# A fused attention and MLP kernel: rules of the build-time planner picked anew, first K and Q in one PSUM bank each, and the second MLP weight loaded at the third group of heads

## Chip, cores and metric

One core of a Trainium2 chip. The metric is the device time of one execution in microseconds (us). Before the change the median of three runs is 724.05 us (723.77 to 724.47).

## What is computed

Softmax attention over 2048 rows with 32 heads of 20 columns, an MLP with the Mish activation, and a gate per row that mixes the two. All inputs are bf16.

```python
x = A_x                                          # 1 x 2048 x 640
g = sigmoid((x * gate_w).sum(-1, keepdims=True))
q, k, v = split(x @ A_wqkv)                      # 32 heads, 20 columns each
p = softmax(q @ k.T * 20 ** -0.5)
a = (p @ v) @ A_wo
h = x @ B_w1 + B_b1
b = (h * tanh(softplus(h))) @ B_w2
return g * a + (1 - g) * b
```

## The kernel before

Heads go in blocks of four (p = 0 to 7) and query rows in chunks of 512 (qc = 0 to 3): 32 "groups" of one block and one chunk. In a group the keys come in 16 "sets" of 128 rows. A set has four score matmuls, one per head, on 32 rows of the array each, so up to four of them run side by side. The scores lie transposed (keys on the partitions) in PSUM, one bank of 512 columns per head and set.

The exponential is taken in two ways. ScalarE takes most: `emit_exp` (L1315) turns two or three neighbouring banks into bf16 in the ring E. VectorE takes the rest by a power trick (`power_of`, L474): one multiply-add into int16 whose bits are a bf16 power of two. Such a set gets two further copies, shifted by an integer add on VectorE (`shift`, L605) or GpSimd (`part`, L573), which are multiplied with scaled values VD. So a set on VectorE costs three value products (`emit_pv`, L1358) instead of one. Values are summed over all sets of a group in bank 7 and normalised (`normalise`, L1380 to L1410), and stored to `o_dram`.

Between scores and values TensorE is given "chains": projections of Q, K and V, both MLP products and the output projection, in pieces of four 32-column matmuls (`product`, L638), each chain with a start and a due time in units of groups.

The order on each engine is made when the program is built: a planner steps through a model of the engines and writes out the instructions in the order in which its engines become free (`step_pe`, `step_act`, `step_dve`, `step_pool`). On the chip each engine runs its list in order and waits on semaphores. The planner's thresholds are fields of `rule`; the table PLAN (L175 to L228) changes them as groups pass: `prog[0]` is the number of sets drawn, over 16, and an entry at 5.0 takes effect at the sixth group. Some of the fields: LOW (how little recent PE work counts as dry), DQ, DQ3, DQ4 (how many powers may queue on VectorE), NOPEN and LEAD (how many sets VectorE may hold open and take of a group), PS and PB (which shifts go to GpSimd, up to which backlog), WAIT1 and WAIT2 (priorities on VectorE), MERGE (two powers in one instruction).

Loads go through two DMA queues: SyncE's (nearly all) and, in the opening, ScalarE's. SyncE issues in order, with eight semaphores in rotation, so that an issue waits until the one eight places before it has landed. In the opening (L315 to L343) the first rows of x, the first K and Q weights (`load_first`, `w_top`) and V weights (`wv0`) are loaded, then the rest of x, weight strips `ws`, `wv`, the MLP's first weight in tiles `w1t`, and at L343 its second weight `w2_sb` (1920 KB; the profile calls the tile w_sb). Behind that on SyncE's queue come zeros for `o_dram` (L1500), the padding rows of K to `k_dram` (L708), Q and K strips to DRAM (L745) and the loads of each group's query tile qT from `q_dram` (L780).

The first projections are written out by hand (L1456 to L1492): transposes of x through banks 0, 3, 6, 2, then K and Q for the first 512 rows, each as ten matmuls of 256 columns into two banks (K 1 and 4, Q 5 and 0), after which VectorE copies one half and ScalarE the other. The first scores need both halves of Q.

At the end, `normalise` of the last group sets `closing`, and while it is set VectorE takes only work of the first priority (L1735).

Of the kernel before, what the change touches and what calls it, by code (L numbers as in the profile page):

```python
# [64 lines left out]
def kernel(  # L65
# [109 lines left out]
    PLAN = {  # L175
        0.0: {'AHEAD': 5000.0, 'BEHIND': 6000.0, 'D2': 1.0, 'DQ': 2, 'DQ3': 0, 'DQ4': 0, 'ETIGHT': 1, 'HEAT': 0.7, 'HROOM': 100.0, 'KEEP3': 3, 'LEAD': 5, 'LOW': 0.5, 'MARGIN': 0.0, 'MERGE': 0, 'NEAR': 99, 'NOPEN': 5, 'PAIR': 0, 'PB': 3000.0, 'PS': 0, 'PVMAX': 4, 'Q3': 3, 'ROOM': 200.0, 'SWTH': 250.0, 'TWO': 9, 'VF': 0, 'VMIN': 1, 'WAIT1': 0.0, 'WAIT2': 6000.0, 'WAITU': 0.0},
        0.5: {'DQ4': 1, 'NEAR': 9, 'WAIT2': 100000.0},
        1.5: {'DQ3': 3, 'ETIGHT': 0, 'HEAT': 0.9, 'VMIN': 3},
# [1 line left out]
        2.5: {'AHEAD': 1000.0, 'Q3': 2},  # L180
        3.5: {'AHEAD': 2000.0, 'NEAR': 7, 'Q3': 3, 'SWTH': 520.0, 'WAIT1': -2000.0},
        4.0: {'MARGIN': 30.0, 'NEAR': 99, 'PVMAX': 2, 'VF': 2, 'VMIN': 1},
        4.5: {'ETIGHT': 1, 'TWO': 2, 'VMIN': 3},
        5.0: {'KEEP3': 1, 'LEAD': 4, 'LOW': 0.47, 'NOPEN': 4, 'Q3': 1, 'SWTH': 600.0, 'WAIT2': 3000.0},
        5.5: {'HROOM': -100.0, 'KEEP3': 3, 'LOW': 0.53, 'NEAR': 12, 'PVMAX': 3, 'VMIN': 2},
        6.0: {'PVMAX': 2},
        6.5: {'HEAT': 0.7, 'PS': 2},
        7.0: {'DQ3': 2, 'NOPEN': 5, 'TWO': 9, 'VMIN': 1},
        7.5: {'PB': 6000.0},
        8.0: {'LEAD': 6, 'WAIT2': 30000.0},  # L190
        8.5: {'HROOM': 100.0, 'MERGE': 1, 'NEAR': 9, 'Q3': 3, 'VF': 0, 'WAITU': -200000.0},
        9.0: {'D2': 0.5, 'HEAT': 0.8, 'MERGE': 0, 'WAITU': 100000.0},
        9.5: {'AHEAD': 3000.0, 'MERGE': 1, 'SWTH': 250.0, 'WAIT1': 0.0},
        10.0: {'PVMAX': 4, 'VF': 2},
        10.5: {'HEAT': 0.9},
        11.0: {'KEEP3': 1, 'ROOM': 300.0},
        11.5: {'KEEP3': 2, 'ROOM': 100.0},
        12.0: {'D2': 0, 'DQ': 1, 'LOW': 0.41, 'MERGE': 0, 'SWTH': 450.0},
        12.5: {'NOPEN': 3, 'Q3': 1},
        13.0: {'Q3': 3},  # L200
        14.0: {'HROOM': -200.0, 'LOW': 0.47, 'WAIT2': 100000.0},
        14.5: {'NOPEN': 2},
        15.0: {'HEAT': 0.7},
        15.5: {'HEAT': 0.9},
        16.0: {'DQ3': 0, 'DQ4': 0, 'HROOM': -100.0},
        17.0: {'PB': 3000.0},
        17.5: {'D2': 0.5, 'PB': 6000.0, 'TWO': 2},
        18.0: {'ROOM': 200.0},
        19.0: {'LOW': 0.6, 'NOPEN': 5},
        19.5: {'DQ3': 2, 'DQ4': 3, 'ETIGHT': 0, 'KEEP3': 1, 'LOW': 0.53, 'TWO': 1},  # L210
        20.0: {'DQ4': 1, 'MARGIN': 60.0, 'MERGE': 1, 'TWO': 2, 'WAIT1': -2000.0, 'WAITU': 0.0},
        20.5: {'NEAR': 99, 'PB': 3000.0, 'SWTH': 380.0},
        21.0: {'DQ4': 2, 'KEEP3': 3, 'NEAR': 7, 'PVMAX': 3},
        21.5: {'ETIGHT': 1, 'MERGE': 0, 'PB': 6000.0, 'Q3': 2, 'WAIT2': 30000.0},
        22.0: {'HROOM': 0.0, 'ROOM': 100.0},
        23.0: {'HROOM': -200.0, 'TWO': 1},
        23.5: {'PVMAX': 2},
        24.0: {'MARGIN': 30.0, 'NOPEN': 2, 'TWO': 9},
        25.0: {'NOPEN': 4, 'PB': 1500.0, 'PVMAX': 4, 'ROOM': 200.0, 'SWTH': 520.0, 'WAIT2': 100000.0},
        25.5: {'LEAD': 5, 'PB': 3000.0, 'WAIT2': 3000.0},  # L220
        26.0: {'HROOM': 100.0, 'ROOM': 100.0, 'TWO': 2},
        26.5: {'HROOM': -200.0, 'PVMAX': 2},
        27.0: {'KEEP3': 2, 'WAIT1': 0.0, 'WAITU': 100000.0},
        27.5: {'LOW': 0.44, 'PVMAX': 4, 'Q3': 3},
        28.0: {'DQ': 2, 'KEEP3': 3, 'MARGIN': 0.0},
        28.5: {'LOW': 0.38, 'TWO': 9, 'WAIT2': 30000.0},
        29.5: {'DQ': 1, 'DQ4': 1, 'NOPEN': 2, 'PS': 0, 'Q3': 1, 'WAIT2': 100000.0},
# [91 lines left out]
    nc.scalar.dma_start(out=w_top[:, :, :], in_=wrows[:, :, D + KTOP : 2 * D])  # L319
# [1 line left out]
    nc.sync.dma_start(out=wv0[:, :, 0 : 4 * DH], in_=wrows[:, :, 2 * D : 2 * D + 4 * DH])
# [43 lines left out]
    def pad_copy(eng, dst, src):  # L365
        eng.tensor_copy(
            out=dst[:, :, :, 0:DH], in_=src.rearrange("p k (h d) -> p k h d", d=DH)
        )
# [1003 lines left out]
    def normalise(G, ready):  # L1372
# [2 lines left out]
        st = {}  # L1375

        def a(t):
            closing[0] = G == NG - 1
# [1 line left out]
            nc.vector.transpose(out=st["T1"][:, :, :].rearrange("p b r -> p (b r)"), in_=acc[:, :])  # L1380

# [97 lines left out]
    qT[0] = qTb[0]
    h_ = QC // 2  # L1480
    for w, dst, two in ((wkp, kT[0], (1, 4)), (wqp, qT[0], (5, 0))):
        for kt in range(KT):
            for h in range(2):
                nc.tensor.matmul(
                    allb[:, two[h], 0:h_],
                    lhsT=w[:, kt, :, :].rearrange("p h d -> p (h d)"),
                    rhs=xT[:, kt, h * h_ : (h + 1) * h_],
                    start=(kt == 0),
                    stop=(kt == KT - 1),
                )  # L1490
        nc.vector.tensor_copy(out=dst[:, 0:h_], in_=allb[:, two[0], 0:h_])
        nc.scalar.copy(out=dst[:, h_:QC], in_=allb[:, two[1], 0:h_])  # L1492
# [389 lines left out]
```

## Time and profile before

| | |
|---|---|
| median of the runs | 724.05 us |
| the profiled execution | 725.01 us |
| its span, from the first to the last instruction | 723.2 us |
| granted TensorE clock, mean | 0.999 |

The profile is of one execution. Busy times are per engine; a line such as L1315 is a line of the kernel before. Rows of a group give line, engine, operation, output<-input, shape and count, then busy time and mean duration of one (ns), then the engine's idle time ahead of them and who ended it. Rows of the timeline give start and length in us, and in brackets the idle time ahead with what ended it. Matmul ends are modelled, so the distance between starts says more than a duration.

### The profile page before, as it was taken

The page shows a single profiled execution, that of the slowest core. Times are in us where ns is not written, and L with a number is a line of the kernel's source. Part 1 is how long each engine was busy: PE and PEld are TensorE (multiplying, and loading weights), DVE is VectorE, ACT ScalarE, POOL GpSimd, SP SyncE. Part 2 cuts the span into 40 slices and gives each one's busy share as a digit, 9 for nine tenths or more (in the row PEclk, how much of TensorE's full clock was granted, in tenths as well). Part 3 has the DMA queues.
Part 4 walks back from the last instruction along what each step waited for, and adds up shares of the span by engine and source line. Part 5 has one row for each costly group of instructions (what it writes and reads, how often), then busy time and mean ns, then how long its engine had stood idle before and what let it go on. Part 6 is the DMA issues. An engine that isn't in the chain of part 4 may idle for free.

```text
span 723.2 us, 24705 instructions
## 1 busy us (share of the span) xinstructions
PE 706.3 (98%) x10256; PEld 232.5 (32%) x10256; DVE 619.6 (86%) x1042; ACT 704.3 (97%) x735; POOL 430.4 (60%) x697
## 2 busy tenths in 40 slices
PE   8899999999999999999999999999999999999997
PEld 4433332222222443332332222222243333333332
DVE  5389999887788779889988899898889988988997
ACT  6899999999999999999999999999999999999996
POOL 2002675565797767778787778667984456663000
PEclk9999999999999999999999999999999999999999
DMA  9511122122321201111131223231231131132111
GB/s 246 178 22 38 30 56 44 33 62 59 85 43 32 68 27 28 14 32 27 50 84 34 41 47 70 60 67 38 44 57 31 34 50 35 29 60 45 20 36 38
DMA packets 123313, 37.87 MB, mean 52 GB/s; under 512 B 90880, under 2 KB 122640, under 8 KB 123200
## 3 DMA queue, kind: packets, MB, share of 16 engines
q1 hardware_dynamic: 121600, 35.80, 22.8%
q8 instruction: 80, 1.31, 0.7%
q10 hardware_dynamic: 1600, 0.49, 0.3%
q14 instruction: 33, 0.27, 0.1%
HBM read 22.29 MB, written 11.48 MB: 47 GB/s over the span
## 4 chain that ended last, share of the span: by engine, by line
PE 62%; ACT 23%; issue 5%; DVE 4%; SPq 2%; DMA 2%; POOL 0%; ACTq 0%; POOLq 0%
PE Sp L1265 22%; ACT E L1315 20%; PE Sp L1358 20%; PE Sp L638 20%; DVE T L474 2%; ACT big L926 1%; DMA w_sb<-in_B_w_dram 1%; DVE T L605 1%; SPq L291 1%; SPq L304 1%; DMA big<-in_A_x_dram 1%; PE Sp L1822 0%; SPq L708 0%; SPq L324 0%; ACT L1315 0%
## 5 line engine op out<-in xcount | busy, mean ns | idle before, releaser
L1315 ACT ACTIVATE E<-Sp 128x1024 bf16<-128x1024 f32 x717 | 672.6, 1077 | 6.3 <-PE Sp L1265 5.9
L573 POOL TENSOR_TENSOR T<-T,step_t 128x256 int32<-128x256 int32 x652 | 401.1, 649 | 107.9 <-PE Sp L1358 71.5
L474 DVE TENSOR_SCALAR T<-Sp 128x512 int16<-128x512 f32 (+1 forms) x587 | 389.1, 686 | 62.3 <-PE Sp L1265 57.7
L1265 PE MATMUL Sp<-qT,kT 32*128 32x512 bf16 x2048 | 290.9, 384 | 8.0 <-ACT E L1315 3.7
L1265 PEld LDWEIGHTS <-kT 32*128 32x128 bf16 x2048 | 74.5, 91 | 267.0 <-issue 262.0
L1358 PE MATMUL Sp<-E,VA 128*21 128x512 bf16 x1456 | 138.0, 383 | 0.4 <-DVE T L1380 0.4
L1401 POOL TENSOR_TENSOR T<-T,rec 128x320 bf16<-128x320 f32 x31 | 25.1, 809 | 167.0 <-DVE rec L1394 140.0
L1358 PE MATMUL Sp<-T,VD 128*21 128x512 bf16 x1184 | 112.2, 382 | 0.5 <-DVE T L605 0.5
L605 DVE TENSOR_SCALAR T<-T 128x2048 int16<-128x2048 int16 x133 | 105.2, 797 | 1.5 <-PE Sp L1358 0.5
L638 PE MATMUL Sp<-xT,w1t 128*32 128x512 bf16 x960 | 76.8, 383 | 0.2
L638 PE MATMUL Sp<-w_sb,big 128*32 128x320 bf16 x1536 | 74.3, 301 | 0.3 <-DVE st L742 0.3
L1358 PEld LDWEIGHTS <-VA 128*21 128x21 bf16 x2048 | 44.4, 90 | 72.5 <-issue 64.5
L1358 PE MATMUL Sp<-T,VA 128*21 128x512 bf16 x592 | 57.4, 383 | 0.0
L638 PE MATMUL Sp<-xT,ws 128*32 128x512 bf16 x720 | 55.9, 382 | 0.5 <-DVE T L474 0.5
L638 PEld LDWEIGHTS <-big 128*32 128x32 bf16 x1536 | 35.4, 96 | 25.9 <-issue 15.8
L1358 PEld LDWEIGHTS <-VD 128*21 128x21 bf16 x1184 | 28.4, 90 | 37.6 <-issue 32.2
L892 DVE TENSOR_SCALAR big<-Sp,b1f 128x512 bf16<-128x512 f32 x48 | 35.6, 742 | 2.1 <-PE Sp L638 1.9
L638 PE MATMUL Sp<-wv,xT 128*32 128x81 bf16 (+2 forms) x960 | 34.6, 258 | 1.3 <-DVE T L474 1.3
L638 PE MATMUL Sp<-wo_sb,od 128*32 128x320 bf16 (+1 forms) x608 | 32.3, 302 | 0.0
L742 DVE CAST st<-Sp 128x512 bf16<-128x512 f32 x36 | 24.5, 681 | 5.3 <-PE Sp L638 5.3
L638 PEld LDWEIGHTS <-w1t 128*32 128x32 bf16 x960 | 19.0, 94 | 26.3 <-issue 22.4
L826 DVE CAST VA<-Sp 128x80 bf16<-128x80 f32 (+2 forms) x48 | 16.2, 372 | 10.1 <-PE Sp L638 10.1
(74 smaller groups left out, 205.7 us busy)
## 6 DMA issues: line engine op xcount, KB each, us to landing
w1t<-in_B_w_dram SPq DMA_DIRECT2D x24, 320.0 KB
q_dram<-st SPq DMA_DIRECT2D x20, 128.0 KB
out_dram<-ot SPq DMA_DIRECT2D x16, 160.0 KB
qT<-q_dram SPq DMA_DIRECT2D x124, 20.0 KB
o_dram<-T SPq DMA_DIRECT2D x120, 20.0 KB
kT<-k_dram SPq DMA_DIRECT2D x28, 80.0 KB
k_dram<-st SPq DMA_DIRECT2D x16, 128.0 KB
big<-in_A_x_dram SPq DMA_DIRECT2D x3, 640.0 KB
```

The lines of the kernel that those rows point to most:

```text
L291: eng.dma_start(out=t[:, :, :], in_=wrows[:, :, c0 : c0 + P])
L474: nc.vector.tensor_scalar(out=dst.bitcast(I16), in0=src, scalar1=inv_sqrt_dh * LOG2E * 128.0, scalar2=127.0 * 128.0 + BETA, op0=ALU.mult, ...
L573: nc.gpsimd.tensor_tensor(out=tile_[:, :].bitcast(I32)[:, k * n : (k + 1) * n], in0=d["T"][:, :].bitcast(I32)[:, k * n : (k + 1) * n], in1 ...
L605: nc.vector.tensor_scalar(out=tile_[:, :].bitcast(I16), in0=d["T"][:, :].bitcast(I16), scalar1=float(SHIFT[i]), scalar2=None, op0=ALU.add,)
L638: nc.tensor.matmul(out_[k : k + 32], lhsT=lhsT[:, k : k + 32], rhs=rhs, tile_position=(0, k), **kw)
L742: nc.vector.tensor_copy(out=res["st"][:, :], in_=ps[:, :])
L826: nc.vector.tensor_copy(out=VA[:, sts[i], h0 : h0 + nh, 0:DH], in_=ps[:, i, 0:n].rearrange("p (h d) -> p h d", d=DH),)
L892: nc.vector.tensor_scalar(out=big[:, slot.tag, (ft % 2) * QC : (ft % 2 + 1) * QC], in0=ps[:, :], scalar1=b1f[:, ft : ft + 1], scalar2=None ...
L1265: nc.tensor.matmul(ps_cols, lhsT=kT[p][32 * t_ : 32 * t_ + 32, j * P : (j + 1) * P], rhs=qT[G][32 * t_ : 32 * t_ + 32, :], tile_position=( ...
L1315: nc.scalar.activation(E[:, x : x + n, :], ps, ACT.Exp, scale=inv_sqrt_dh,)
L1358: nc.tensor.matmul(acc[32 * t_ : 32 * t_ + DH + 1, :], lhsT=lhsT, rhs=rhs, start=(pv_done[G] == 0), stop=(pv_done[G] == pv_total[G] - 1), ...
L1401: nc.gpsimd.tensor_tensor(out=T2[i][:, :].rearrange("p (b r) -> p b r", r=32)[:, :, 0:DH], in0=st["T1"][:, :, 0:DH], in1=st["rec"][:, :].u ...
```

## The change

1. PLAN is replaced whole: all fields of `rule` as before, other values at other groups (52 entries before, 59 after; those at 0.0 and 0.5 are the same).
2. First K and Q: five matmuls of 512 columns each into one bank (6 for K, 2 for Q); VectorE and ScalarE still copy one half each, now out of the same bank.
3. `w_top` moves from ScalarE's queue to SyncE's, `wv0` from SyncE's to ScalarE's, behind Q's weights.
4. `w2_sb` is not loaded in the opening but by an event once more than two groups' sets have been drawn.
5. `closing` is taken out.

```diff
     PLAN = {
...
         0.5: {'DQ4': 1, 'NEAR': 9, 'WAIT2': 100000.0},
-        1.5: {'DQ3': 3, 'ETIGHT': 0, 'HEAT': 0.9, 'VMIN': 3},
-        2.0: {'DQ4': 2, 'NEAR': 5, 'PS': 1, 'ROOM': 100.0, 'VMIN': 2, 'WAITU': 100000.0},
...
+        1.0: {'DQ4': 3, 'VMIN': 2, 'WAITU': 100000.0},
+        1.5: {'DQ4': 2, 'PS': 2, 'PVMAX': 3},
...
     load_first(1, nc.sync)
-    nc.scalar.dma_start(out=w_top[:, :, :], in_=wrows[:, :, D + KTOP : 2 * D])
     load_first(0, nc.scalar)
-    nc.sync.dma_start(out=wv0[:, :, 0 : 4 * DH], in_=wrows[:, :, 2 * D : 2 * D + 4 * DH])
+    nc.sync.dma_start(out=w_top[:, :, :], in_=wrows[:, :, D + KTOP : 2 * D])
+    nc.scalar.dma_start(out=wv0[:, :, 0 : 4 * DH], in_=wrows[:, :, 2 * D : 2 * D + 4 * DH])
...
     load_w1(1)
-    nc.sync.dma_start(out=w2_sb[:, :, :], in_=B_w2.rearrange("(ft p) c -> p ft c", p=P))
...
-    closing = [False]
...
-            closing[0] = G == NG - 1
...
-            closing[0] = False
...
+    sb = [bank_ap(g, [P, QC]) for g in (6, 2)]
     kT[0] = kTb[0]
     qT[0] = qTb[0]
-    h_ = QC // 2
-    for w, dst, two in ((wkp, kT[0], (1, 4)), (wqp, qT[0], (5, 0))):
+    for w, dst, k in ((wkp, kT[0][:, 0:QC], 0), (wqp, qT[0][:, :], 1)):
         for kt in range(KT):
-            for h in range(2):
-                nc.tensor.matmul(
-                    allb[:, two[h], 0:h_],
-                    lhsT=w[:, kt, :, :].rearrange("p h d -> p (h d)"),
-                    rhs=xT[:, kt, h * h_ : (h + 1) * h_],
-                    start=(kt == 0),
-                    stop=(kt == KT - 1),
-                )
-        nc.vector.tensor_copy(out=dst[:, 0:h_], in_=allb[:, two[0], 0:h_])
-        nc.scalar.copy(out=dst[:, h_:QC], in_=allb[:, two[1], 0:h_])
+            nc.tensor.matmul(
+                sb[k][:, :],
+                lhsT=w[:, kt, :, :].rearrange("p h d -> p (h d)"),
+                rhs=xT[:, kt, 0:QC],
+                start=(kt == 0),
+                stop=(kt == KT - 1),
+            )
+        h_ = QC // 2
+        nc.vector.tensor_copy(out=dst[:, 0:h_], in_=sb[k][:, 0:h_])
+        nc.scalar.copy(out=dst[:, h_:QC], in_=sb[k][:, h_:QC])
...
+    def load_w2():
+        nc.sync.dma_start(out=w2_sb[:, :, :], in_=B_w2.rearrange("(ft p) c -> p ft c", p=P))
+
     events = [
+        (lambda t: prog[0] > 2.0, lambda t: load_w2()),
...
-            if it[1] <= t and (it[0] == 0 or not closing[0]) and (it[6] is None or it[6](t)):
+            if it[1] <= t and (it[6] is None or it[6](t)):
```

More of the change, by code (lines that the diff above doesn't have):

```diff
@@ L177 @@
         0.5: {'DQ4': 1, 'NEAR': 9, 'WAIT2': 100000.0},
-        1.5: {'DQ3': 3, 'ETIGHT': 0, 'HEAT': 0.9, 'VMIN': 3},
-        2.0: {'DQ4': 2, 'NEAR': 5, 'PS': 1, 'ROOM': 100.0, 'VMIN': 2, 'WAITU': 100000.0},
[L180 to L227, printed above, removed]
+        1.0: {'DQ4': 3, 'VMIN': 2, 'WAITU': 100000.0},
+        1.5: {'DQ4': 2, 'PS': 2, 'PVMAX': 3},
+        2.0: {'DQ4': 1, 'PS': 1, 'PVMAX': 4, 'VF': 1, 'WAIT1': -2000.0},
+        2.5: {'Q3': 2},
+        3.0: {'DQ3': 2},
+        3.5: {'VF': 2, 'WAIT1': 2000.0, 'WAITU': 0.0},
@@ new lines @@
+        4.0: {'ROOM': 100.0},
+        4.5: {'D2': 0.5, 'ETIGHT': 0, 'MERGE': 1},
+        5.0: {'DQ4': 0, 'LEAD': 4, 'LOW': 0.47, 'MERGE': 0, 'NEAR': 99, 'NOPEN': 4, 'PS': 0, 'Q3': 1, 'SWTH': 600.0, 'VMIN': 3, 'WAIT2': 3000.0},
+        5.5: {'D2': 1.0, 'DQ3': 3, 'MARGIN': 100.0, 'WAIT1': -2000.0},
+        6.5: {'HEAT': 0.9, 'HROOM': -200.0, 'LEAD': 6, 'MARGIN': 0.0, 'PB': 6000.0, 'PS': 1, 'VMIN': 2},
+        7.0: {'MARGIN': 30.0},
+        7.5: {'VMIN': 1},
+        8.0: {'HEAT': 0.8, 'PS': 2, 'PVMAX': 2, 'Q3': 3, 'WAIT2': 100000.0},
@@ new lines @@
+        8.5: {'D2': 0, 'DQ3': 2, 'NEAR': 7},
+        9.0: {'DQ3': 1, 'WAIT2': 3000.0},
+        9.5: {'DQ3': 2, 'HROOM': 0.0, 'PVMAX': 4, 'WAIT1': 2000.0, 'WAIT2': 100000.0},
+        10.0: {'DQ3': 1},
+        10.5: {'MARGIN': 150.0, 'VF': 0},
+        11.0: {'LEAD': 5},
+        11.5: {'D2': 0.5, 'DQ': 1, 'DQ3': 0, 'MARGIN': 0.0, 'PB': 3000.0, 'PVMAX': 3},
+        12.0: {'NOPEN': 3, 'VF': 1},
+        12.5: {'VF': 2},
+        13.5: {'MERGE': 1, 'NOPEN': 4, 'PB': 6000.0, 'SWTH': 380.0},
+        14.0: {'PVMAX': 4, 'TWO': 0},
@@ new lines @@
+        14.5: {'HROOM': -100.0, 'LEAD': 6, 'MERGE': 0, 'PS': 1, 'Q3': 2, 'TWO': 9},
+        15.0: {'PS': 2},
+        15.5: {'D2': 1.0, 'PB': 3000.0},
+        16.0: {'DQ3': 3, 'HEAT': 0.9, 'NEAR': 5, 'NOPEN': 5, 'WAIT2': 30000.0},
+        16.5: {'LEAD': 5},
+        17.0: {'HEAT': 0.8, 'VMIN': 3},
+        17.5: {'D2': 0, 'KEEP3': 1, 'NEAR': 7, 'WAIT1': -2000.0},
+        18.0: {'D2': 1.0, 'HROOM': -200.0, 'KEEP3': 2, 'LOW': 0.5, 'NEAR': 9, 'PVMAX': 2},
+        18.5: {'KEEP3': 3, 'SWTH': 300.0},
@@ new lines @@
+        19.0: {'LOW': 0.6, 'MARGIN': 100.0, 'MERGE': 1, 'VMIN': 1, 'WAIT2': 3000.0},
+        19.5: {'DQ3': 0},
+        20.0: {'Q3': 1},
+        20.5: {'DQ4': 3, 'WAITU': -200000.0},
+        22.0: {'SWTH': 450.0, 'WAIT1': 0.0},
+        22.5: {'AHEAD': 2000.0, 'ETIGHT': 1, 'KEEP3': 2, 'LEAD': 6, 'WAIT2': 100000.0},
+        23.0: {'NEAR': 5, 'Q3': 2},
+        23.5: {'WAITU': 100000.0},
+        24.0: {'DQ3': 2, 'DQ4': 1},
+        24.5: {'NEAR': 7, 'PVMAX': 3, 'TWO': 1},
+        25.0: {'ETIGHT': 0, 'ROOM': 200.0},
@@ new lines @@
+        25.5: {'DQ4': 0},
+        26.0: {'Q3': 3},
+        26.5: {'D2': 0.5, 'DQ': 2, 'ETIGHT': 1, 'HROOM': 0.0, 'LOW': 0.56, 'WAIT2': 3000.0},
+        27.0: {'ETIGHT': 0, 'Q3': 2, 'WAIT2': 6000.0},
+        27.5: {'AHEAD': 5000.0, 'LOW': 0.41, 'MARGIN': 30.0, 'WAITU': -200000.0},
+        28.0: {'DQ': 3, 'LOW': 0.53, 'MARGIN': 60.0, 'MERGE': 0, 'ROOM': 100.0},
+        28.5: {'AHEAD': 1000.0, 'DQ3': 1, 'KEEP3': 1, 'MARGIN': 100.0, 'PVMAX': 2, 'SWTH': 300.0},
+        29.0: {'MARGIN': 30.0, 'PVMAX': 4, 'SWTH': 380.0},
@@ L228 @@
+        29.5: {'NOPEN': 2, 'TWO': 0, 'VF': 1},
+        30.5: {'DQ': 1, 'ETIGHT': 1, 'LOW': 0.41, 'PS': 1, 'VF': 2},
+        31.0: {'PS': 0, 'PVMAX': 2},
+        31.5: {'BEHIND': 3000.0, 'DQ4': 1, 'ETIGHT': 0, 'HROOM': 100.0, 'LEAD': 5},
     }
```

## The prediction

> **What bounds the kernel now.** I read the first page, then the stretches, then the chain of waits, then single pieces of the timeline.
>
> ```profile
> span 723.2 us, 24705 instructions
> PE 706.3 (98%) x10256; PEld 232.5 (32%) x10256; DVE 619.6 (86%) x1042; ACT 704.3 (97%) x735; POOL 430.4 (60%) x697
> PE 62%; ACT 23%; issue 5%; DVE 4%; SPq 2%; DMA 2%; POOL 0%; ACTq 0%; POOLq 0%
> ```
> ```profile
> 300.00:400.00 100.00, 99.23 (x1456) 30.94 (x1452) 88.44 (x143) 99.84 (x109) 78.61 (x126) 1.00 0.20 42
> 600.00:700.00 100.00, 99.58 (x1541) 33.80 (x1541) 91.83 (x154) 100.00 (x109) 42.34 (x68) 1.00 0.20 38
> 661.00:700.00 39.00, 38.92 (x618) 13.54 (x614) 37.33 (x65) 39.00 (x43) 0.73 (x1) 1.00 0.17 38
> ```
>
> The columns of the stretches are length, then busy time (with instructions) of PE, PE's weight loads, DVE, ACT and POOL, then the granted clock, DMA share and GB/s. TensorE and ScalarE are both full at a granted clock of 1.00, and the chain passes from one to the other: 62% on PE, 23% on ACT. A shorter order has to take work from both. VectorE stands close behind (92 of 100 us, and 37.3 of the last 39).
>
> **The exponentials (the rules).** From here on I compare the order of instructions in the two built programs. The new rules give 150 sets to VectorE's power trick instead of 148, so ScalarE gets 688 exponentials of 1024 columns (693 now), 24 of 1536 (23) and none of 512 (1).
>
> ```profile
> L1315 ACT ACTIVATE E<-Sp 128x1024 bf16<-128x1024 f32 x693 | 644.4, 1064 | 6.2 <-PE Sp L1265 5.9 <-PE Sp L1358 0.2
> L1315 ACT ACTIVATE E<-Sp 128x1536 bf16<-128x1536 f32 x23 | 34.2, 1487 | 0.1
> L1315 ACT ACTIVATE E<-Sp 128x512 bf16<-128x512 f32 x1 | 0.7, 667 | 0.0
> ```
>
> Consecutive ones overlap, so busy time over count is the price: 644.4/693 = 0.93 us for 1024 columns, 1.49 for 1536, 0.67 for 512. ScalarE's sum is -5 x 0.93 + 1.49 - 0.67 = -3.83 us.
>
> **TensorE (the rules).** Up to four small matmuls run side by side, so I count slots of four and read the distance between starts.
>
> ```profile
> 59.83 0.40 PE L1358 MATMUL Sp<-T,VD 128*21 128x512 bf16 x4
> 60.06 0.39 PE L1358 MATMUL Sp<-E,VA 128*21 128x512 bf16 x4
> 60.27 0.39 PE L1358 MATMUL Sp<-T,VA 128*21 128x512 bf16 x4
> 60.59 0.39 PE L1265 MATMUL Sp<-qT,kT 32*128 32x512 bf16 x4
> 60.92 0.29 PE L638 MATMUL Sp<-wv,xT 128*32 128x240 bf16 x4
> ```
>
> A slot of values after a slot of values comes 0.21 to 0.23 us later (I use 0.22), but the way into the scores costs 0.32 (60.27 to 60.59) and the way out 0.33. A visit to the scores therefore costs 0.32 + 0.33 - 0.22 = 0.43 us. The new order has 728 score slots instead of 739; 13 of those it loses stood directly behind another score slot (15 left of 28), so it has 2 visits more (713 for 711). Two more sets with two shifted copies each add 4 slots of values (812 for 808). Filler slots (projections, MLP, output) keep their number. Sum: -13 x 0.22 + 2 x 0.43 + 4 x 0.22 = -1.1 us.
>
> Which saving counts? Where PE sets the pace 1.1, where ACT does 3.8. I weigh them by the chain, 62 to 23: 0.73 x 1.1 + 0.27 x 3.83 = 1.8 us. Ends: -1.1 and -3.8.
>
> **The opening.** Loads and first projections of now:
>
> ```profile
> 1.65 0.43 SPq L298 DMA_DIRECT2D wf<-in_A_wqkv_dram  x1
> 1.65 0.46 ACTq L319 DMA_DIRECT2D w_top<-in_A_wqkv_dram  x1
> 2.12 0.53 SPq L321 DMA_DIRECT2D wv<-in_A_wqkv_dram  x1
> 6.06 0.22 DVE L1474 COPY wkp<-w_top 128x240 bf16<-128x240 bf16 x1
> 7.20 0.27 DVE L366 COPY wqp<-wf 128x400 bf16<-128x400 bf16 x1 [0.91 <-DMA wf<-in_A_wqkv_dram]
> 7.52 1.27 PE L1484 MATMUL Sp<-xT,wqp 128*128 128x256 bf16 x10
> 8.71 0.42 DVE L1491 CAST qT<-Sp 128x256 bf16<-128x256 f32 x1 [0.71 <-PE Sp L1484]
> 8.82 0.37 ACT L1492 CAST qT<-Sp 128x256 bf16<-128x256 f32 x1 [0.77 <-PE Sp L1484]
> 9.24 0.40 PE L1265 MATMUL Sp<-qT,kT 32*128 32x512 bf16 x4 [0.46 <-ACT qT L1492]
> ```
>
> Five matmuls of 512 columns stand for ten of 256: the same columns, cost 0. But the two halves of Q are now copied side by side out of two banks (8.71 and 8.82). In the changed program both lie in one bank, and ScalarE's copy waits for VectorE's: 8.82 + 0.42 + 0.37 + two hand-overs of about 0.05 (9.19 to 9.24) = 9.71 for the first score instead of 9.24, +0.48 us. K's pair is serial too, but its copies lie under Q's matmuls (1.27 us). The Trainium skill, "PSUM — Partial Sum Buffer", section on bank collisions, says that ScalarE and VectorE must not read one bank at the same partitions at once, reads against reads included. By it the 0.48 cannot be won back by dropping the wait; without it the copies would overlap and cost 0. The trace, with two banks, cannot show a collision.
>
> w_top moves from ScalarE's queue to SyncE's, behind wf: issued at 2.12 instead of 1.65. Q's weights move up a place on ScalarE's queue, and the V weights go behind them. K now waits for w_top. If it comes no later, 0 (PE has no idle before 7.52, so Q's earlier weights win nothing). If it comes as late as the last of the four today (7.20), VectorE copies at 7.20 instead of 6.06, and K and Q run 1.1 us later. I take +0.3, two thirds of the 0.47 by which the issue moves. Everything behind the first score is in order on PE, so I let the opening's +0.8 stand; 0 if a later load hides it.
>
> **w_sb.** It is on the chain now:
>
> ```profile
> 18.91 10.30 DMA w_sb<-in_B_w_dram
> SPq L708 <- DMA w_sb<-in_B_w_dram: 3.6, 1, 3.6
> 32.76 1.39 SPq L780 DMA_DIRECT2D qT<-q_dram  x4
> 35.21 0.71 PE L1265 MATMUL Sp<-qT,kT 32*128 32x512 bf16 x2 [0.84 <-DMA qT<-q_dram]
> 36.88 1.94 ACT L1315 ACTIVATE E<-Sp 128x1024 bf16<-128x1024 f32 x2 [1.40 <-PE Sp L1265]
> ```
>
> The transfer keeps SyncE's fourth K store waiting 3.6 us, this the second group's query load behind it (32.76), TensorE waits 0.84 us for that, and ScalarE 1.40. Without w_sb ahead of it the load is issued some 4 to 5 us earlier and both waits go: -1.4, the longer of them, as exponentials are what runs behind. Next late would be VectorE's powers for the same scores; if those hold PE, the gain is 0.
>
> In its new place the load's single issue stands on SyncE behind the first group's four stores, ahead of a K store, a Q store, the fourth group's four query loads and the second group's four stores.
>
> ```profile
> 54.10 2.89 SPq L1434 DMA_DIRECT2D o_dram<-T  x4
> 48.87 10.43 ACT L1315 ACTIVATE E<-Sp 128x1024 bf16<-128x1024 f32 x11
> ```
>
> That is about 57 us; with 10.3 us it lands by 67.3, and the query load (2.4 us from 32.76 to 35.2) by about 70 to 72. In the new order w_sb stands at the 47th exponential and the fourth group's first score at the 72nd: 25 x 0.95 = 23.7 us later, about 81. The cover is some 9 us of scores and values, cost 0; were it gone, the rest of the 10.3 would fall on TensorE. Its own reader comes much later, with the MLP.
>
> **The tail.** Removing "closing" lets VectorE take other work in the last normalisation; there is none left: 0.
>
> ```profile
> 712.51 2.46 DVE L605 TENSOR_SCALAR T<-T 128x2048 int16<-128x2048 int16 x4
> 713.40 0.10 PEld L1358 LDWEIGHTS <-VA 128*21 128x21 bf16 x4 [0.98 <-issue]
> 715.46 0.72 DVE L1380 STREAM_TRANSPOSE T<-Sp 128x512 f32<-128x512 f32 x1 [0.50 <-PE Sp L1358]
> ```
>
> Now four shifts are left for VectorE at the end, and PE waits. In the new order the last two are issued before the last exponential, and output slots fill the wait. I take -0.3 (half the first gap), between -0.8 and +0.3 (two filler slots too many).
>
> **Sum.** -1.8 + 0.5 + 0.3 - 1.4 - 0.3 = -2.7 us on this execution's 725.01 us (span 723.2 and 1.8 around it): 722.3. The runs shown have a median 0.96 below it, 724.05; on that scale 721.3.
>
> **Rivals.**
> 1. *ScalarE alone sets the pace* and PE's waits shrink with it: -3.8 + 0.8 - 1.4 - 0.8 = -5.2, 718.8. For it: ACT at 99.8 to 100 in every stretch. Against: the chain is on PE for 62%.
> 2. *VectorE comes late* (slower). Its work grows:
>
> ```profile
> L474 DVE TENSOR_SCALAR T<-Sp 128x512 int16<-128x512 f32 x582 | 383.1, 681 | 62.1 <-PE Sp L1265 57.5 <-POOL T L573 0.6
> L474 DVE TENSOR_SCALAR T<-Sp 128x1024 int16<-128x1024 f32 x5 | 6.1, 1216 | 0.2 <-PE Sp L1265 0.2
> L605 DVE TENSOR_SCALAR T<-T 128x2048 int16<-128x2048 int16 x133 | 105.2, 797 | 1.5 <-PE Sp L1358 0.5
> ```
>
> 578 single powers for 582 (0.66 each), 11 pairs for 5 (1.22), 135 shifts for 133 (0.79): -2.6 + 7.3 + 1.6 = +6.3 us. A power that is late keeps a bank, and so the scores behind it. If all 6.3 reach the path where the savings should be, the time is 6.3 + 0.8 - 1.4 - 0.3 = +5.4, 729.5; with half, +2.3, 726.3. It decides from about 2.4 of the 6.3 on (+2.4 - 0.9 = +1.5). For it: 92% busy late in the kernel. Against: 62 us of idle before its powers.
> 3. *The opening gives it back*: w_top as late as 7.20 and PE held by the powers where w_sb held it: -1.8 + 0.5 + 1.1 + 0 - 0.3 = -0.5, 723.5, no change.
> 4. *w_sb only moves its stall*: the fourth group's query load waits for it. With no cover, 10.3 us less what the old place cost: 721.3 + 10.3, 731.6. The Trainium skill, "DMA: Bandwidth & Descriptors", section on queues and rings, has each ring consumed in order, so what is issued behind w_sb does wait; the trace's 3.6 us of SyncE agrees. Against: the 9 us of cover.
>
> **How the numbers follow.** Forecast 0.42 (719.5 to 722.6), rival 1 0.20, rival 3 0.15, rival 2 0.20, rival 4 0.03. A change under 0.2% (1.45 us) can't be told from none in this kernel's runs. Faster (below 722.6): 0.42 + 0.20 = 0.62. Same: 0.15 and a little of rival 2, 0.17. Slower: 0.21. The range goes from 717.4 (PE's and ACT's savings fall in different stretches and add, and the opening loses nothing: -1.1 - 3.8 - 1.4 - 0.3 = -6.6) to 726.3 (rival 2 with half).
>
> **What would show it.** Right: first exponential at 10.2 to 10.6 instead of 9.67; no wait of TensorE for qT near 35; w_sb landing before 70 and nobody waiting for it; ACT's busy sum near 700. Wrong: TensorE waiting for VectorE's tiles (powers or shifts) more than now, PE's busy share below 97%, or a first exponential after 11.

## The result, and the profile after

The changed kernel takes 720.8 us (median of five, 720.6 to 721.32) and the kernel before, in the same comparison, 724.05 (723.77 to 728.24). The ratio is 0.9945 with an interval of 0.9928 to 0.9962: faster by 3.25 us. The forecast was 721.3, faster. The profiled execution of the changed kernel took 720.62, its span is 718.8.

The first page of the changed kernel (span, busy times, chain by engine), then its stretches with the columns as in the prediction:

```profile
span 718.8 us, 24738 instructions
PE 704.8 (98%) x10262; PEld 234.9 (33%) x10262; DVE 626.2 (87%) x1046; ACT 700.2 (97%) x730; POOL 440.9 (61%) x705
PE 76%; ACT 15%; issue 4%; DVE 3%; DMA 1%; SPq 0%; ACTq 0%; DVEq 0%
```
```profile
300.00:400.00 100.00, 99.68 (x1447) 31.25 (x1439) 91.40 (x150) 99.91 (x110) 77.81 (x124) 1.00 0.18 43
600.00:700.00 100.00, 99.26 (x1545) 35.39 (x1544) 89.40 (x147) 99.74 (x105) 62.99 (x100) 1.00 0.20 39
661.00:700.00 39.00, 38.82 (x635) 14.78 (x632) 33.17 (x58) 39.00 (x40) 17.34 (x28) 1.00 0.17 39
```

ScalarE has 4.1 us less to do (704.3 before), and the chain passes from 62 to 23 (PE to ACT) over to 76 to 15: the exponentials stand in the way less often. In the last 39 us VectorE has 33.2 us of work where it had 37.3, and GpSimd, almost idle there before (0.73), has taken 17.3. The groups of ScalarE and VectorE:

```profile
L1320 ACT ACTIVATE E<-Sp 128x1024 bf16<-128x1024 f32 x688 | 640.4, 1079 | 5.1 <-PE Sp L1270 3.4 <-PE Sp L1363 1.1
L1320 ACT ACTIVATE E<-Sp 128x1536 bf16<-128x1536 f32 x24 | 36.6, 1523 | 0.2 <-PE Sp L1270 0.2
```
```profile
L479 DVE TENSOR_SCALAR T<-Sp 128x512 int16<-128x512 f32 x578 | 383.0, 683 | 55.5 <-PE Sp L1270 49.4 <-POOL T L578 1.4
L610 DVE TENSOR_SCALAR T<-T 128x2048 int16<-128x2048 int16 x135 | 106.7, 795 | 2.3 <-PE Sp L1363 1.0
L479 DVE TENSOR_SCALAR T<-Sp 128x1024 int16<-128x1024 f32 x11 | 13.3, 1211 | 0.4 <-PE Sp L1270 0.4
```

VectorE's sum went from 619.6 to 626.2, and its idle time ahead of the single powers fell from 62.1 to 55.5: the additional work went into idle time.

The start of the changed kernel, on VectorE, ScalarE and PE:

```profile
6.83 0.22 DVE L1477 COPY wkp<-w_top 128x240 bf16<-128x240 bf16 x1 [0.34 <-DMA w_top<-in_A_wqkv_dram]
9.55 0.42 DVE L1494 CAST qT<-Sp 128x256 bf16<-128x256 f32 x1 [0.72 <-PE Sp L1486]
```
```profile
10.01 0.37 ACT L1495 CAST qT<-Sp 128x256 bf16<-128x256 f32 x1 [0.77 <-DVE qT L1494]
10.86 3.77 ACT L1320 ACTIVATE E<-Sp 128x1024 bf16<-128x1024 f32 x4 [0.48 <-PE Sp L1270]
```
```profile
10.43 0.40 PE L1270 MATMUL Sp<-qT,kT 32*128 32x512 bf16 x4 [0.99 <-ACT qT L1495]
```

K's weights now wait for w_top, Q's two copies run one behind the other (9.55 to 9.97, 10.01 to 10.38), and the first score stands at 10.43 (9.24 before).

SyncE's queue around the new place of w_sb, and its longest wait there (us in total, times, longest):

```profile
59.00 0.49 SPq L1538 DMA_DIRECT2D w_sb<-in_B_w_dram  x1
59.60 0.77 SPq L750 DMA_DIRECT2D k_dram<-st  x1
62.78 0.33 SPq L750 DMA_DIRECT2D q_dram<-st  x1
70.89 1.42 SPq L785 DMA_DIRECT2D qT<-q_dram  x4
```
```profile
SPq L785 <- DMA q_dram<-st: 18.3, 11, 7.7
```

The store of Q that was issued behind w_sb lands only at 70.9, and the fourth group's query loads wait 7.7 us for it. TensorE's scores go on without a gap (they stand at 0.8 to 1.1 us from one another from 66 to 83 us): nobody waits for SyncE.

The end, on PE and ScalarE:

```profile
710.36 0.65 PE L1363 MATMUL Sp<-E,VA 128*21 128x512 bf16 x4
710.95 1.26 PE L1829 MATMUL Sp<-wo,O 128*128 128x320 bf16 x8
```
```profile
698.81 11.77 ACT L1320 ACTIVATE E<-Sp 128x1536 bf16<-128x1536 f32 x12
```

The same on ScalarE in the kernel before:

```profile
699.24 15.21 ACT L1315 ACTIVATE E<-Sp 128x1024 bf16<-128x1024 f32 x16
```

The exponentials run without a gap to 710.58, and nothing of VectorE's shifts is left behind them: the last normalisation's first transpose starts at 711.05, 0.47 us later. Before, it started at 715.46, 1.0 us after the last exponential (714.45).

### The profile page after: what moved, and what is told of

It is laid out like the page before. It is cut to its first block, busy times and chain, and to the rows that moved or that the text cites. A ratio compares the mean times of both kernels' runs of the same rounds, so it can differ in the third digit from the quotient of the medians.

```text
span 718.8 us, 24738 instructions
## 1 busy us (share of the span) xinstructions
PE 704.8 (98%) x10262; PEld 234.9 (33%) x10262; DVE 626.2 (87%) x1046; ACT 700.2 (97%) x730; POOL 440.9 (61%) x705
## 4 chain that ended last, share of the span: by engine, by line
PE 76%; ACT 15%; issue 4%; DVE 3%; DMA 1%; SPq 0%; ACTq 0%; DVEq 0%
PE Sp L1270 27%; PE Sp L643 25%; PE Sp L1363 24%; ACT E L1320 15%; DVE T L479 1%; DMA kT<-k_dram 1%; DMA w_top<-in_A_wqkv_dram 1%; DVE T L610 0%; PE Sp L1486 0%; SPq L776 0%; DVE T L1384 0%; DVE st L747 0%; DVE VD L430 0%; SPq L324 0%; PE Sp L653 0%
## 5 line engine op out<-in xcount | busy, mean ns | idle before, releaser
L1320 ACT ACTIVATE E<-Sp 128x1024 bf16<-128x1024 f32 (+1 forms) x712 | 668.5, 1094 | 5.4 <-PE Sp L1270 3.6
L578 POOL TENSOR_TENSOR T<-T,step_t 128x256 int32<-128x256 int32 x660 | 409.7, 654 | 156.7 <-PE Sp L1363 92.1
L479 DVE TENSOR_SCALAR T<-Sp 128x512 int16<-128x512 f32 (+1 forms) x589 | 395.9, 693 | 55.9 <-PE Sp L1270 49.8
L1270 PE MATMUL Sp<-qT,kT 32*128 32x512 bf16 x2048 | 285.9, 384 | 6.0 <-ACT E L1320 2.0
L1270 PEld LDWEIGHTS <-kT 32*128 32x128 bf16 x2048 | 76.7, 91 | 264.1 <-issue 258.6
L610 DVE TENSOR_SCALAR T<-T 128x2048 int16<-128x2048 int16 x135 | 106.7, 795 | 2.3 <-PE Sp L1363 1.0
L1405 POOL TENSOR_TENSOR T<-T,rec 128x320 bf16<-128x320 f32 x31 | 27.1, 875 | 89.8 <-DVE rec L1398 78.3
L643 PE MATMUL Sp<-w_sb,big 128*32 128x320 bf16 x1536 | 76.4, 301 | 0.5 <-DVE T L479 0.4
L643 PEld LDWEIGHTS <-xT 128*32 128x32 bf16 x960 | 17.9, 96 | 16.3 <-issue 14.3
```

What stands on the lines that cost most here:

```text
L479: nc.vector.tensor_scalar(out=dst.bitcast(I16), in0=src, scalar1=inv_sqrt_dh * LOG2E * 128.0, scalar2=127.0 * 128.0 + BETA, op0=ALU.mult, ...
L578: nc.gpsimd.tensor_tensor(out=tile_[:, :].bitcast(I32)[:, k * n : (k + 1) * n], in0=d["T"][:, :].bitcast(I32)[:, k * n : (k + 1) * n], in1 ...
L610: nc.vector.tensor_scalar(out=tile_[:, :].bitcast(I16), in0=d["T"][:, :].bitcast(I16), scalar1=float(SHIFT[i]), scalar2=None, op0=ALU.add,)
L643: nc.tensor.matmul(out_[k : k + 32], lhsT=lhsT[:, k : k + 32], rhs=rhs, tile_position=(0, k), **kw)
L1270: nc.tensor.matmul(ps_cols, lhsT=kT[p][32 * t_ : 32 * t_ + 32, j * P : (j + 1) * P], rhs=qT[G][32 * t_ : 32 * t_ + 32, :], tile_position=( ...
L1320: nc.scalar.activation(E[:, x : x + n, :], ps, ACT.Exp, scale=inv_sqrt_dh,)
```

## The experiments

**Where TensorE's time goes.** For the profiles in the table I took the distances between the starts of TensorE's slots from the first score to the last matmul, subtracted for each the median distance between slots of these two kinds in the profile of before, and added up what remains as waits, in three parts. All numbers are worked out from the profiles' rows, in us; e12 and e13 are the unchanged kernels, profiled once more.

```
kernel                   first score  slots   waits to 36.5  to last 12 us  last 12 us  last matmul
before                       9.24     688.22      2.49           16.72         2.00       718.67
before again (e12)           9.73     688.22      0.70           16.76         2.00       717.43
w_sb late alone (e3)         9.19     688.22      0.83           18.36         2.01       718.62
opening alone (e4)          10.46     688.22      0.51           17.00         2.00       718.20
opening and w_sb (e5)       10.10     688.22      0.50           18.34         2.01       719.18
rules alone (e6)             9.27     686.83      1.97           18.83         0.51       717.41
after                       10.43     686.83      0.50           15.99         0.51       714.26
after again (e13)           10.37     686.83      0.51           16.20         0.51       714.41
```

The rows add up: 10.43 + 686.83 + 0.50 + 15.99 + 0.51 = 714.26. The experiments refer to this table.

**The parts of the change by themselves.** The first runs take one part out of the kernel after, or put one into the kernel before.

e1: the kernel after with the opening of before (both queues and two banks).

```diff
+    nc.scalar.dma_start(out=w_top[:, :, :], in_=wrows[:, :, D + KTOP : 2 * D])
...
-    nc.sync.dma_start(out=w_top[:, :, :], in_=wrows[:, :, D + KTOP : 2 * D])
-    nc.scalar.dma_start(out=wv0[:, :, 0 : 4 * DH], in_=wrows[:, :, 2 * D : 2 * D + 4 * DH])
+    nc.sync.dma_start(out=wv0[:, :, 0 : 4 * DH], in_=wrows[:, :, 2 * D : 2 * D + 4 * DH])
...
-    for w, dst, k in ((wkp, kT[0][:, 0:QC], 0), (wqp, qT[0][:, :], 1)):
+    for w, dst, two in ((wkp, kT[0], (1, 4)), (wqp, qT[0], (5, 0))):
...
```

> The changed kernel with the opening of before (two banks each for first K and Q, w_top on ScalarE's queue, wv0 on SyncE's); rules and w_sb as changed; every order behind the opening is the changed kernel's. My theory (the first score comes 1.2 us later in the changed kernel, 10.43 for 9.24, and all behind it keeps that): 1.2 us faster than the changed kernel, about 719.6, first score near 9.3. Rival (a later load hides the opening): the same as the changed kernel, 720.8.

Measured 720.76 us (719.34 to 721.13), 0.9925 of before (0.9902 to 0.9949): no difference from 720.8. In its profile the first score came 0.90 us earlier than after, and at 180 us 0.51 of that was left. Then the weight loads of its scores show a wait for a K tile that the kernel before doesn't have, here in e1 and in the kernel after:

```profile
186.64 0.09 PEld L1270 LDWEIGHTS <-kT 32*128 32x128 bf16 x1 [1.35 <-DMA kT<-k_dram]
```
```profile
186.15 0.09 PEld L1270 LDWEIGHTS <-kT 32*128 32x128 bf16 x1 [0.36 <-DMA kT<-k_dram]
```

In the new order a score needs a K tile about when its load lands. Behind this wait e1 is 0.48 us later than after. It is not that an earlier start waits longer for a fixed arrival: SyncE issues the eight K loads earlier in e1 too (from 179.29 us, 179.80 in after), and the tile came later all the same. By the account of the table the wait is 0.45 us in after, 0.5 in e13, 0.9 in e2, whose first score is the latest of all (10.71), 1.4 in e1 and 2.0 in e6 and e10, and e8 keeps 0.39 of its lead of 0.71 to the end. So what e1's opening wins was lost here in this execution; that it is always lost isn't shown.

e2: the kernel after with w_sb loaded in the opening.

```diff
+    nc.sync.dma_start(out=w2_sb[:, :, :], in_=B_w2.rearrange("(ft p) c -> p ft c", p=P))
...
-        (lambda t: prog[0] > 2.0, lambda t: load_w2()),
...
```

> The changed kernel with w_sb loaded in the opening as before; nothing else moves. My theory: TensorE waits for qT near 36 again, 1.4 us slower than the changed kernel, about 722.2. Rival (the powers held PE there anyway): 720.8, no change.

Measured 721.02 (720.65 to 723.28), 0.9939 (0.9916 to 0.9961). The later load wins 0.2 us in the kernel after by the medians, which is no more than the runs scatter. Its profile has a wait of 0.3 us at 35.65 where after has none.

e3: the kernel before with w_sb at the third group alone; the order of the four computing engines stays that of before.

```diff
-    nc.sync.dma_start(out=w2_sb[:, :, :], in_=B_w2.rearrange("(ft p) c -> p ft c", p=P))
...
+        (lambda t: prog[0] > 2.0, lambda t: load_w2()),
```

> The kernel before with w_sb alone moved to the third group of heads. My theory: the waits of 0.84 (TensorE) and 1.40 us (ScalarE) near 35 go, 1.4 us faster, about 722.6. Rival (no gain by itself, something else is late at the same place): 724.0.

Measured 724.06 (723.52 to 725.27), 0.9977 (0.9961 to 0.9994) of the kernel before, which had a median of 725.03 beside it. The wait near 35 us is gone, but in the profile the 1.5 us are lost again at 258 us (18.36 for 16.72 in the fourth column). What happens there is told below.

e4: the kernel before with the new opening alone (queues and single banks).

```diff
-    nc.scalar.dma_start(out=w_top[:, :, :], in_=wrows[:, :, D + KTOP : 2 * D])
...
+    nc.sync.dma_start(out=w_top[:, :, :], in_=wrows[:, :, D + KTOP : 2 * D])
...
-    for w, dst, two in ((wkp, kT[0], (1, 4)), (wqp, qT[0], (5, 0))):
+    for w, dst, k in ((wkp, kT[0][:, 0:QC], 0), (wqp, qT[0][:, :], 1)):
...
```

> The kernel before with the changed opening alone. My theory: first score at 10.4 instead of 9.24, 1.2 us slower, about 725.2; but since w_sb's stall near 35 hangs on the transfer and not on TensorE, up to half of it may be hidden there, 724.6. Rival (hidden whole): 724.0.

Measured 724.56 (724.29 to 725.85), 0.9986 (0.9971 to 1.0001). Its profile has no wait for qT near 35 us although w_sb is loaded in the opening, which the forecast's account of that wait did not allow for.

The next runs take the rules alone and the opening in its halves.

e5: the kernel after with the old rules (the whole PLAN of before), which is the opening and the late w_sb on the kernel before, with `closing` out.

```diff
     PLAN = {
...
-        1.0: {'DQ4': 3, 'VMIN': 2, 'WAITU': 100000.0},
-        1.5: {'DQ4': 2, 'PS': 2, 'PVMAX': 3},
+        1.5: {'DQ3': 3, 'ETIGHT': 0, 'HEAT': 0.9, 'VMIN': 3},
+        2.0: {'DQ4': 2, 'NEAR': 5, 'PS': 1, 'ROOM': 100.0, 'VMIN': 2, 'WAITU': 100000.0},
...
```

> The changed kernel with the rules of before: the order of before, with the changed opening and w_sb at the third group. My theory (opening +1.2, w_sb -1.4): about 723.8. What is then left to the rules is 720.8 - 723.8 = -3.0. Rival (opening and w_sb give the whole gain): 721.

Measured 724.48 (724.14 to 726.01), 0.9999 (0.9989 to 1.0010) of before: without the rules nothing is won.

e6: the kernel before with the new rules (the whole PLAN of after) alone.

```diff
     PLAN = {
...
-        1.5: {'DQ3': 3, 'ETIGHT': 0, 'HEAT': 0.9, 'VMIN': 3},
-        2.0: {'DQ4': 2, 'NEAR': 5, 'PS': 1, 'ROOM': 100.0, 'VMIN': 2, 'WAITU': 100000.0},
+        1.0: {'DQ4': 3, 'VMIN': 2, 'WAITU': 100000.0},
+        1.5: {'DQ4': 2, 'PS': 2, 'PVMAX': 3},
...
```

> The kernel before with the new rules alone, opening and w_sb as before. My theory: the rules are worth 3.0 us, about 721.0. The forecast's own size for them was -1.8 and -0.3 in the tail, 722.0; the rival that ScalarE alone sets the pace had -3.8 and -0.8, 719.5; the rival of a late VectorE would make it slower than 724.

Measured 720.56 (720.11 to 723.74), 0.9948 (0.9932 to 0.9964) of before. That is the ratio of the whole change (0.9945). This kernel keeps `closing`, and its last 12 us are those of after (0.51 in the table): taking `closing` out is worth 0 there, as forecast. Its profile was taken in the longest of these executions, 723.74; what cost it 3 us is shown below.

e7: the kernel after with K and Q in two banks each; the queues stay new. e8: the kernel after with the queues of before; the single banks stay.

```diff
-    for w, dst, k in ((wkp, kT[0][:, 0:QC], 0), (wqp, qT[0][:, :], 1)):
+    for w, dst, two in ((wkp, kT[0], (1, 4)), (wqp, qT[0], (5, 0))):
...
```

> The changed kernel with two banks each for first K and Q again, the changed queues kept. My theory: only the serial copy goes, -0.5 us of the opening's 1.2, first score near 9.95, about 720.3. Rival (the bank costs nothing, the queue all): 720.8, first score 10.4.

```diff
+    nc.scalar.dma_start(out=w_top[:, :, :], in_=wrows[:, :, D + KTOP : 2 * D])
...
-    nc.sync.dma_start(out=w_top[:, :, :], in_=wrows[:, :, D + KTOP : 2 * D])
...
```

> The changed kernel with the queues of before in the opening (w_top on ScalarE's, wv0 on SyncE's), one bank each kept. My theory: -0.7 us of the opening's 1.2, first score near 9.75, about 720.1. Rival (the queue order costs nothing, the late first score of that one profile came from x arriving late): 720.8, and the first score still near 10.4 in some runs.

Measured 721.14 (720.23 to 724.27) and 720.4 (719.88 to 721.42), ratios 0.9951 (0.9928 to 0.9975) and 0.9941 (0.9929 to 0.9953). Neither differs from after by more than the runs scatter. The first scores in their profiles, two banks and then old queues:

```profile
9.97 0.40 PE L1270 MATMUL Sp<-qT,kT 32*128 32x512 bf16 x4 [0.46 <-ACT qT L1495]
```
```profile
9.72 0.40 PE L1270 MATMUL Sp<-qT,kT 32*128 32x512 bf16 x4 [0.99 <-ACT qT L1495]
```

With two banks the wait of the first score is 0.46 instead of 0.99 and it stands 0.46 earlier than in after: the serial copies cost what was forecast. With the old queues it stands 0.71 earlier, so by this profile w_top behind wf costs 0.7 rather than 0.3. One profile is a rough measure of that: the first score stands at 9.19 to 9.73 in five profiles with the old opening (before, e12, e3, e6, e1) and at 10.08 to 10.71 in seven with the new one (after, e13, e2, e4, e5, e10, e11), with medians of 9.27 and 10.39.

**Which engine sets the pace.** Work was added to one engine, spread over the whole kernel. e10: the kernel after issues the first score matmul of every 16th visit to the scores twice, into the same bank (44 slots more). e11: after every 16th exponential ScalarE makes a copy of 32 columns that nobody reads.

```diff
+            if k == 0 and it_no[0] % 16 == 0:
+                score(ps[:, k, :], G, j, t_)
+                s_left[G] += 1
```

> The changed kernel with one score matmul issued twice in every sixteenth visit to the scores (44 more, same rows, same bank, so each takes a slot of its own of 0.22 us): 9.7 us more work for TensorE, none for the others, order otherwise the same. The forecast's weights (PE sets the pace for 0.73): +7, about 728. ScalarE alone sets the pace: +2 at most, 723. Both full at once, so that any delay of either reaches the end: +9.7, 730.5.

```diff
...
+        n_exp[0] += 1
+        if n_exp[0] % 16 == 0:
+            nc.scalar.copy(out=idle_w, in_=zero_w)
```

> The changed kernel with a small copy (128x32) on ScalarE after every sixteenth exponential (44 more, about 0.2 us each): 8.9 us more for ScalarE, none for the others. The forecast's weights (ACT sets the pace for 0.27): +2.4, about 723.2. ScalarE alone sets the pace: +8.9, 729.7. Both full at once: +8.9 too, told apart by the run with more work on TensorE.

Measured 726.98 (726.53 to 730.23) and 723.69 (722.94 to 724.03), so +6.2 and +2.9 us over after. TensorE's slots grew by 10.07 us by the account of the table; the visits with a second issue take 0.53 us instead of 0.32 (medians), which is 9.2 us for 44. Two exponentials with a copy between them start 1.012 us apart and two without 0.905 (medians of that profile), so the 44 copies add 44 x 0.107 = 4.7 us and not the 8.9 expected, whatever their own duration. The time follows both engines by about 0.6 to 0.7 (6.2/10.07 or 6.2/9.2, and 2.9/4.7). Were ScalarE alone the bound, e10 would have cost next to nothing. The chain's 15% for ACT is too small a weight for added work of ScalarE. How much of work that is taken away comes out, these two don't show, since added work can also make an engine the bound where it wasn't.

**How constant the terms are.** Both kernels, unchanged, were profiled a second time.

> The kernel before, unchanged, profiled once more: how constant are the terms that the forecast priced from one execution? If w_sb's stall is a property of the program, the stretch around the first wait for qT (near 35 us) again costs some 1.55 us and the span is 722.5 to 724. If the stall depends on when the transfers of that execution arrive, the wait near 35 us is shorter or gone (under 0.8 us), and the span is nevertheless 722.5 to 724, since the time that is not lost there is lost at a later wait. Start of the first score 9.24 in both.

> The kernel after, unchanged, profiled once more: first score at 10.43 and first exponential at 10.86 again if the delay of the opening is a property of the program (between 10.2 and 10.6 if the 0.3 above the forecast was chance). The wait of a score matmul for the k load near 186 us: about 0.4 us if it depends on the program alone, anywhere from 0 to 1.6 us if on when the transfer of that execution arrives. Span 717.5 to 720.

e12 took 723.77 us, its span is 722.0. TensorE around the second group's first scores, SyncE's queue ahead of them, and the chain by engine, all of e12:

```profile
33.31 0.99 PE L1358 MATMUL Sp<-E,VA 128*21 128x512 bf16 x12
34.23 0.39 PE L1265 MATMUL Sp<-qT,kT 32*128 32x512 bf16 x4
34.55 0.61 PE L638 MATMUL Sp<-xT,ws 128*32 128x512 bf16 x8
```
```profile
18.66 0.76 SPq L343 DMA_DIRECT2D w_sb<-in_B_w_dram  x1
...
29.15 1.55 SPq L708 DMA_DIRECT2D k_dram<-kT  x4
30.80 1.40 SPq L780 DMA_DIRECT2D qT<-q_dram  x4
```
```profile
PE 63%; ACT 26%; issue 5%; DVE 4%; DMA 0%; POOL 0%; ACTq 0%
```

The query load is issued at 30.80 instead of 32.76, TensorE waits for nothing, and the 2% each of SyncE's queue and of DMA are gone from the chain. Compared instruction by instruction with the first profile, this one starts 0.49 us later, is 1.29 us ahead behind the wait, and stays 1.24 to 1.26 us ahead to the end. So the wait was real and reached the end, but it belonged to that execution. The expectation that a later wait would take it was wrong. The other profiles bear this out: with w_sb in the opening the wait at this place is 1.54 us in before, 0.8 in e6, 0.3 in e2 and 0 in e12 and e4, and in the seven profiles with the late load (after, e13, e1, e3, e5, e7, e8) there is none. e13 took 720.74; its first score stands at 10.37, and to the end it is never more than 0.15 us from the first profile of after.

**Half clock.** Here are the stretches around 258 us of e3 and of e12, which have the same order of instructions on TensorE; the number behind POOL's is the granted clock:

```profile
254.50:258.00 3.50, 2.48 (x25) 0.67 (x26) 3.38 (x6) 3.49 (x4) 2.26 (x4) 0.97 0.08 29
258.00:261.30 3.30, 3.30 (x42) 1.04 (x46) 1.98 (x4) 2.29 (x4) 2.82 (x5) 0.52 0.02 5
261.30:265.00 3.70, 3.70 (x61) 1.09 (x57) 3.65 (x6) 3.70 (x4) 0.60 (x2) 1.00 0.13 44
```
```profile
254.50:258.00 3.50, 2.48 (x29) 0.70 (x21) 3.13 (x6) 3.49 (x4) 2.01 (x4) 1.00 0.13 47
258.00:261.30 3.30, 3.30 (x64) 1.30 (x61) 3.29 (x6) 3.30 (x5) 3.06 (x5) 1.00 0.03 5
```

For 3.4 us (257.8 to 261.2 by the trace's clock) e3's TensorE works at half its clock, and in the second stretch ScalarE gets 2.29 us of work instead of 3.30. e3 goes into it 0.25 us ahead of e12 and comes out 1.18 behind: 1.43 us, kept to the end. e5's profile has the same stretch at the same place (clock 0.54). In e6, and at the same place in e10, it stands elsewhere, behind a long wait for kT; the score and the stretch after it, of e6:

```profile
187.94 0.39 PE L1272 MATMUL Sp<-qT,kT 32*128 32x512 bf16 x1 [1.59 <-DMA kT<-k_dram]
```
```profile
189.50:193.00 3.50, 3.50 (x36) 0.63 (x28) 0.90 (x3) 2.36 (x3) 0.00 (x0) 0.53 0.00 0
```

Wait and stretch together cost e6 3.0 us against after, which is why its profiled execution took 723.74 and its median 720.56.

Why e3 and not e12, with one order of instructions? In all profiles the stretches at full clock last whole multiples of 3.413 us: 252.6 us in e3 and e5 (74 of them), 184.3 in e6 and e10 (54), 716.8 in before (210). So the traces read as if the clock were set anew every 3.413 us, on a grid that lies differently over the program in each execution (full clock starts 3.9 to 7.1 us into the span). Ahead of 258 us TensorE's order is thin: three scores stand behind waits (255.11, 255.71 and 256.55 us in e3). In e3 and e5 this thin stretch falls whole into one piece of the grid, in which TensorE is busy for 2.38 and 2.39 us of 3.41, and the clock drops behind it. In e12, e4 and before the grid cuts it, no piece has less than 2.71, and the clock holds. Busy time alone doesn't decide: e8 has a piece of 2.38 at 519.7 us and keeps its clock.

The Trainium skill, "TensorE: Matmul & The Clock Gate", Part 1 on the HAM clock gate, has the clock fall to half after an idle window of about 3.4 us, and the window runs free of the kernel. The half rate, the length and the free grid agree with these rows. The condition doesn't, as the page states it: in the piece ahead of the drop TensorE was busy for 2.38 of 3.41 us by the profile.

## Why the forecast came out right, point by point

Direction, size and range held. That the sum came so near is partly luck: it was 1.4 too high for w_sb and 1.6 too low for the rules and the tail, and these errors cancel. The table above gives the terms from the execution of before without the wait near 35 us (e12: 723.77) to after (720.62):

```
                                     forecast    measured
opening: first score later             +0.8       +0.70, less 0.20 that waits to 36.5 us take up
rules: slots and waits in between      -1.8       -1.39 slots, -0.77 waits = -2.16
tail (last 12 us)                      -0.3       -1.49
w_sb                                   -1.4        0
sum                                    -2.7       -3.15
```

- **The rules** carry the gain: alone they give 0.9948 (e6), and without them 0.9999 is left (e5). The count of ScalarE's exponentials and VectorE's powers held (-4.1 and +6.6 us against -3.83 and +6.3), and so did the slots (-1.39 against -1.1). The step that failed in size is the weight by the chain, 0.73 x 1.1 + 0.27 x 3.83, together with the tail that was priced beside it: -2.1 by the forecast, -3.65 in the runs.
- **The tail** is the term with the largest error. The forecast looked at the gap behind the last exponential, and that did shrink by 0.5. But most of the waits lay ahead of it, in the last score visits: the row of the kernel before (e12) at 711.85, and the shift at the end of it:

```profile
711.85 0.37 PE L1265 MATMUL Sp<-qT,kT 32*128 32x512 bf16 x1 [0.37 <-ACT E L1315]
...
713.18 0.40 PE L1358 MATMUL Sp<-T,VD 128*21 128x512 bf16 x4 [0.20 <-DVE T L605]
```

  Here TensorE has no filler slots left and waits for ScalarE and VectorE in turn. In the new order output slots are kept for these places (709.38 and 709.87 in after), and 2.00 us of waits become 0.51 in all the kernels of the table with the new rules. The upper bound of the gain, -0.8, was too near.
- **w_sb.** The step that failed is "without w_sb ahead of it ... both waits go: -1.4". The mechanism is as described, and the late load does take the wait away, but with the early load it is 1.54 us in the profile shown (1.29 + 0.25) and 0 to 0.8 in the four others, 0.5 on average. And it was counted against a median that didn't contain it: the 0.96 us by which the profiled 725.01 stood above 724.05 is no constant of the scale but for the most part this very wait. Taking off the wait and then the 0.96 takes it off twice. The lowest of the three runs shown, 723.77, is what an execution without the wait takes (e12). By e3's interval the late load wins 0.4 to 2.8 us on the kernel before (0.0006 and 0.0039 of 725), but that isn't shown to be the load's: more of the executions of before beside it ran at a lowered clock (14 of 23 at 0.997 or less, 5 of 12 of e3), and among those at 0.998 or more the medians are 724.04 and 723.75.
- **The opening.** The single banks cost 0.46 (forecast 0.48). For w_top the 0.3 was too low: 0.71 by e8, within its bounds of 0 and 1.1. Together that is 1.2, and the medians of the first scores stand 1.1 apart; the 0.70 of the table is low because e12's first score is the latest of the five with the old opening. The first exponential stood at 10.86, outside the 10.2 to 10.6 that would have shown the step right, though below 11. That the opening's loss then stands to the end was not quite so: a wait for x near 19 us takes up some of it (e1's lead on after falls there from 0.90 to 0.51). What reaches the time lies within the scatter: e1, e7 and e8 are no faster than after.
- **The new place of w_sb** is covered, as forecast: SyncE waits and TensorE does not. The query loads are issued by 72.3 and the fourth group's first score stands at 80.56 (forecast about 81). Rival 4 falls. One reading in it does not hold: SyncE's 3.6 us in the opening are a wait for w_sb's own landing, eight places later, and say nothing of the order in a queue; what agrees with that order is the store of Q, issued at 62.78 behind w_sb and waited for until 70.89.
- **Rival 1**, ScalarE alone as the bound, falls by e10 (+6.2 us for work of TensorE). **Rival 2** falls: VectorE's idle time took the 6.6 us, and TensorE's waits for powers and shifts fell, not rose. **Rival 3** expected the opening to give everything back; on the table's terms it gives back about 0.5 of 3.65.

An obvious rival is the clock: is the gain only that the new order is spared half clock? Of the 59 executions of before that stand beside e3, e5 and e10, 30 have a mean granted clock of 0.997 or less; of the 35 of after, e1, e2, e6, e7 and e8 one has. But among those at 0.998 or more the medians are 724.09 and 720.81, so the gain of some 3.3 us is there without it.

Left open: why the waits between 36 us and the end shrink by 0.77. It is a difference of larger numbers. Waits of over 0.25 us fall from 12.4 us (22 in e12) to 7.5 (17 in after), the largest that goes being one of 1.13 for a power at 43 us, and smaller ones grow by 4.0. By the profile's list TensorE's waits for powers and shifts fall from 2.9 to 0.7 us and those for ScalarE from 3.7 to 2.0 (the tail's among them), and those for the transposes of `normalise` grow from 0.4 to 1.3. The two kernels' orders differ throughout, and no run takes them apart.

## What to carry to other kernels

A wait at a transfer is a term of one execution until a second profile of the same program shows it again: compare the profiled time with the median first, and don't take a stall off both. Where two engines are full, price the end of the kernel by itself: in the last few us there is no filler left, and an order that kept some back won 1.5 us there, about as much as the slots it saved in the 700 us before. A gain at the start has to pass every later wait for a load, and those vary from one execution to the next by as much as it is worth: here 0.9 us at the first score was 0.5 behind the first such wait and gone behind the second, in one profile.

## What the runs showed that was not expected

A run of TensorE at half clock for 3.4 us in the middle of a busy kernel costs 1.43 us. The order sets where TensorE is thin, but whether an execution drops its clock there is not set by the program alone: two of the five profiles with the old order have it at 258 us, three don't. Together with the wait near 35 us it makes the executions of one kernel fall into groups some 1.5 us apart: of e3's twelve, eight lie between 723.5 and 724.5 and four between 724.9 and 725.3, and the profiled one with the half clock is among the four. All four have a mean granted clock of 0.996 or 0.997, and seven of the eight have 0.999.
